# Two of twelve pairs of attention heads move beside the first output layer

## The chip, the cores and the metric

The kernel runs on one core of one Trainium2 chip. Its time is the device time of one execution in microseconds (us); three runs of the kernel before gave 1255.74 to 1256.49 us, with a median of 1256.26 us. The engines of the core are named as the profile names them: PE is the tensor engine (PEld its weight loads), DVE the vector engine, ACT the scalar engine, POOL GpSimd, and SP the engine that issues most of the DMAs.

## The reference

Attention over 4 batches, 12 heads, 448 tokens and a head size of 64 in float32, with scores capped by a tanh, and behind it two expert layers over all 1792 tokens with 768 columns and 2048 hidden columns:

```python
scores = cap * tanh((q @ k.T / sqrt(64)) / cap)
attn = exp(scores - max) / (sum + 1e-9);  x = attn @ v        # as [1792, 768]
h = x @ moe_w_in;   x = (h * cos(h)) @ moe_w_out
h = maximum(x @ moe2_w_in, 0);   out = (h * h) @ moe2_w_out
```

The weights come as float64, q, k and v as float32.

## The kernel before

**Precision.** Each float32 operand is kept as a high part, rounded to float32r, and a low part, the rest. A product of two such operands is three matmuls (`mm3`): high by high, high by low and low by high.

**Windows and stages.** The four batches are taken in two windows of two. A window is eight stages in a row, each a call of `layer` or `layer_out` with 288 expert matmuls of 128 x 448: `layer(True)` makes half of the first layer's hidden columns with the cosine, `layer_out(o_part)` multiplies them into partial sums that wait in the tiles `part`, a second `layer(True)` and `layer_out(o_x)` do the same for the other half and add, which gives x again as two halves; then `layer(False)`, `layer_out(o_part)`, `layer(False)` and `layer_out(o_y)` do the second expert layer and write the output. In this document a stage of the first window is meant where nothing else is said; its eight stages begin at 138.73, 213.97, 273.37, 333.91, 433.60, 527.45, 620.34 and 699.80 us after the span's start, and the next window begins at 768.92 us.

**Banks of PSUM.** `layer(True)` turns over four banks, the two of `bM` and the two of `bA`. `layer_out` uses `bM` alone, one bank for each of the two batches, and so does `layer(False)`. The copy of a finished bank of `layer_out` is on ACT: L613 in `o_part`, L618 in `o_x`, where DVE then adds the first half's sum (L619), rounds (L620), and POOL makes the low half (L621).

**Weights.** All stages of the first window make float32 of the float64 words, one unit after another: 8 units of 128 x 768 in a `layer`, 12 units of 128 x 512 in a `layer_out`. A unit's steps are a DMA (`w_raw`, SP), an absolute value on ACT (L143), four operations on DVE (L144, L145, L146, L149) and an addition on POOL (L152); then its high part on ACT (L166) and its low part on POOL (L169), which the tensor engine waits for. `w_next` begins each unit: it writes the float32 form of the next unit to DRAM for the later window (`w_keep`), splits the next unit, loads the words four units ahead, and queues the steps of the unit three ahead, which `w_step` then issues one by one between the matmuls. In a stage `layer_out`, with 24 matmuls a unit and six steps, that is one step every third matmul.

**Attention.** It works on pairs of heads, 12 pairs for each window. The first window's pairs (0 to 11) come ahead of everything. The second window's pairs (12 to 23) run beside stages of the first window. `a_steps` makes a list of 6 x 12 + 5 = 77 steps of them. Counted from a pair's own first step (six after the last pair's), step 0 holds eight transposes, the making of the halves of q and k, and the loads for the next pair; steps 2 to 5 a score group each, four matmuls, with its tanh; steps 3 to 6 the exponentials with their halves ph (ACT, L394) and pl (DVE, L396), step 3 also the halves of v; steps 5 to 8 the product with v, six matmuls each, which add up in `bA`; step 9 the division by the sums on DVE (`a_out`); step 10 writes the result to DRAM. That makes 48 instructions of the tensor engine a pair. `layer(True)` can't have a product with v beside it, since it uses `bA` itself.

**The order.** All engines get their instructions in the order in which the Python code runs; nothing reorders them. `mm` counts the expert matmuls in `rate[0]` and issues one step of the list `side` after each `rate[1]` of them. In `window` the list is set ahead of `layer_out(o_x)`, with a rate of (1152 - 20) // 77 = 14, so the steps spread over `layer_out(o_x)`, `layer(False)`, `layer_out(o_part)` and `layer(False)`; what is left over runs ahead of the last stage. `later` and `tick` put off the second and third part of a tile's cosine or square by one tile.

Of the kernel before, what the change touches and what calls it, by code (L numbers as in the profile page):

```python
# [21 lines left out]
CAP_MAX = 40.0  # L22
# what a pair of heads makes room for, after each of its four chunks, of the first weights' steps
W_SLOTS = [("act", "dve"), ("act", "dve"), ("pool", "split"), ("dma", "act", "dve")]
# [4 lines left out]
def tile_softcap_attention_moe_cos_moe_relu2(  # L29
# [11 lines left out]
):  # L41
    # Every float32 operand x of a product is carried as hi + lo, both float32r:
    # hi is x rounded to float32r, lo = x - hi, and hi*hi + hi*lo + lo*hi keeps float32's accuracy.
    nc = tc.nc
# [52 lines left out]

# [1 line left out]
    # They come as float64, in two words. The first batch rounds them to float32 from the words,  # L99
    # keeps that in DRAM for the batches after it, and splits it; later batches load and split it.  # L100
    wseq = []
# [27 lines left out]
    def w_bits(i):  # L129
        # The steps that make float32 of the words, the last of them the rounding; or the load of what they made.  # L130
        if i >= wend[0]:
            return []
        n = wseq[i % NW].shape[1] * P
        wf[i] = t = wf_p.tile([P, NCC * P], F32, name="wf", tag="wf")
        f, u = t[:, :n], t[:, :n].bitcast(U32)
        if i >= NW:
            nc.sync.dma_start(out=f, in_=wkeep[i % NW])
            return []
        r = wraw.pop(i)
        rd = wf_p.tile([P, NCC * P], U32, name="wd", tag="wd", bufs=1)  # L140
        lo, hi = r[:, :n, 0], r[:, :n, 1]
        return [
            lambda: nc.scalar.activation(out=f, in_=r.bitcast(F32)[:, :n, 1], func=AF.Abs),  # L143
            lambda: nc.vector.tensor_scalar(out=rd[:, :n], in0=lo, scalar1=2.0 ** -29, scalar2=None, op0=ALU.mult),  # L144
            lambda: nc.vector.tensor_scalar(out=f, in0=f, scalar1=2.0 ** -15, scalar2=None, op0=ALU.max),  # L145
            lambda: nc.vector.tensor_scalar(  # L146
                out=u, in0=u, scalar1=3, scalar2=0x3FFFFFFF, op0=ALU.logical_shift_left, op1=ALU.bitwise_and
            ),
            lambda: nc.vector.scalar_tensor_tensor(  # L149
                out=u, in0=hi, scalar=0xC0000000, in1=u, op0=ALU.bitwise_and, op1=ALU.bitwise_or  # L150
            ),
            lambda: nc.gpsimd.tensor_tensor(out=u, in0=u, in1=rd[:, :n], op=ALU.add),  # L152
        ]
# [26 lines left out]
    def w_start():  # L180
        # The first units' steps, each with the engine that it holds.
        i = wpos[0]
        early = [("dma", partial(w_raw, i)), ("dma", partial(w_raw, i + 1))]
        for j in range(i, i + 4):
            # the steps exist only once the load before them does
            early += [(e, partial(w_bit, j, k)) for k, e in enumerate(("act",) + 4 * ("dve",) + ("pool",))]
# [33 lines left out]

# [1 line left out]
    # Partition r < 64 holds tokens 4r..4r+3, partition r >= 64 tokens 256+3(r-64)..+2;  # L222
    # column 128c + r of a transposed tile is the c-th token of partition r.
    def rows_a(t, b, h, n=1):
# [4 lines left out]

    # The pairs before the first layer find the tiles of g free; later pairs run beside the layers.  # L230
    raws, vraws, qkts = {}, {}, {}
# [13 lines left out]

    # the second pair's loads need not wait for the first's to be consumed
    def wide_view(t):
# [5 lines left out]
    def a_load(n):  # L253
# [5 lines left out]
        else:  # L259
            qr = at_p.tile([P, 4, 2, D], F32, name="qr", tag="qr")  # L260
        # the fourth chunk of k holds one head's tokens in each half, and zeros beside them
        eq, ek = (nc.sync, nc.sync) if n else (nc.scalar, nc.gpsimd)
# [66 lines left out]
    def a_score(n, g):  # L329
# [10 lines left out]
        else:  # L340
            # rows: the high parts of k twice, beside q's high and low parts; then k's low part
            q2, k2, kl = qkts[n]
# [191 lines left out]

# [1 line left out]
    pend = []  # L536
# [93 lines left out]
    def y_tr(b, d, y):  # L630
# [13 lines left out]
        )  # L644

    def window(w, steps=(), weave=None):
        layer(True, weave)
        layer_out(o_part)
        layer(True)
        side[:] = steps  # L650
        if steps:
            rate[:] = [0, (4 * FB * NCC * 3 * WB - 20) // len(steps)]
        layer_out(o_x)
        layer(False)
        layer_out(o_part)
        layer(False)
        while side:
            side_step()
        rate[:] = [0, 0]
        layer_out(o_y(w), w)  # L660

    # |score| <= |cap|, so exp(score) needs no shift while |cap| <= CAP_MAX; and 1e-9 beside the
    # shifted sum, which is at least 1, is below half a unit in its last place. For a larger cap
    # all is computed once more, from scores shifted by their row's maximum.
    def general():
# [19 lines left out]

    # Products of zeros that nothing reads: the tensor engine's clock doubles only after it has been busy a while.
    def busy(n):
# [67 lines left out]
```

## Time and profile before

| | us |
|---|---|
| median of three runs | 1256.26 |
| lowest, highest run | 1255.74, 1256.49 |
| span of the profiled execution (first to last instruction) | 1255.5 |
| PE busy | 1203.0 (96%) |
| DVE busy | 787.4 (63%) |
| ACT busy | 674.4 (54%) |
| POOL busy | 529.9 (42%) |

The busy shares are means over stages that have different limits; the table by stage in the rows below tells them apart. The profiled execution is told by its span alone; the median of the runs is 0.8 us above it. A matmul's duration in the profile overlaps the next one's, so the pace of the tensor engine is read from the length of a stage and not from the mean duration of a matmul.

### The profile page before, as it was taken

How to read it: one execution, taken by the hardware profiler on the slowest of the kernel's cores; microseconds unless marked ns; L12 is line 12 of the kernel's file. 1: busy time of each engine (PE TensorE's matmuls, PEld its weight loads, DVE VectorE, ACT ScalarE, POOL GpSimd, SP SyncE). 2: the span in 40 equal slices, each digit the busy share in tenths (PEclk: the TensorE clock that was granted, in tenths of full speed). 3: DMA queues.
4: the chain of work that ended last, by engine and by line, in shares of the span. 5: the costliest groups of instructions: out<-in, count | busy, mean ns of one | idle time of the engine just before them, and what ended most of it. 6: DMA issues, size and time to landing. Idle time of an engine off the chain costs nothing.

```text
span 1255.5 us, 16524 instructions
## 1 busy us (share of the span) xinstructions
PE 1203.0 (96%) x5931; PEld 1038.6 (83%) x5931; DVE 787.4 (63%) x1123; ACT 674.4 (54%) x1068; POOL 529.9 (42%) x358
## 2 busy tenths in 40 slices
PE   8888889999999899999999989999999999999996
PEld 6555678998878778888888879999999999999996
DVE  6999999669988998777787773530353232013222
ACT  7787576346766688876687434531362144114311
POOL 3555545555566654344443554222224432222221
PEclk9999999999999999999999999999999999999999
DMA  4333243454344443345533465112111211221132
GB/s 106 88 93 97 61 158 122 160 197 143 120 123 139 152 131 122 115 129 153 168 133 111 151 199 145 44 44 66 64 38 51 65 62 35 58 72 46 43 94 49
DMA packets 145308, 130.17 MB, mean 104 GB/s; under 512 B 54816, under 2 KB 124720, under 8 KB 145216
## 3 DMA queue, kind: packets, MB, share of 16 engines
q1 hardware_dynamic: 144224, 128.72, 33.5%
q8 instruction: 49, 0.80, 0.3%
q14 instruction: 43, 0.35, 0.1%
q10 hardware_dynamic: 928, 0.23, 0.1%
q0 software_dynamic: 64, 0.07, 0.0%
HBM read 95.55 MB, written 33.42 MB: 103 GB/s over the span
## 4 chain that ended last, share of the span: by engine, by line
PE 68%; DVE 19%; issue 6%; ACT 3%; DMA 2%; POOL 1%; SPq 1%; DVEq 0%; ACTq 0%; POOLq 0%
PE bM L524 55%; PE bA L524 6%; PE bA L407 3%; PE bS L348 2%; DVE wd L144 2%; DVE g L392 2%; DVE wf L145 2%; DVE xl L96 1%; DVE u L554 1%; DVE st L422 1%; DVE xx L434 1%; DVE wf L146 1%; DVE wf L149 1%; DVE g L570 1%; POOL wf L152 1%
## 5 line engine op out<-in xcount | busy, mean ns | idle before, releaser
L524 PE MATMUL bM<-g,wh 128*128 128x448 f32 x1536 | 445.7, 370 | 6.2 <-DVE part L626 5.1
L169 POOL TENSOR_TENSOR wl<-wf,wh 128x512 fp32r<-128x512 f32 (+1 forms) x160 | 256.3, 1602 | 336.1 <-DVE wh L168 300.3
L524 PEld LDWEIGHTS bM<-g,wh 128*128 128x128 f32 x1536 | 286.7, 189 | 36.0 <-ACT wh L166 4.8
L524 PE MATMUL bM<-g,wl 128*128 128x448 f32 x768 | 284.0, 370 | 5.8 <-POOL wl L169 5.7
L152 POOL TENSOR_TENSOR wf<-wf,wd 128x512 uint32<-128x512 uint32 (+1 forms) x80 | 133.2, 1665 | 234.6 <-issue 129.2
L524 PE MATMUL bM<-xh,wl 128*128 128x448 f32 x576 | 212.2, 368 | 2.7 <-POOL wl L169 2.7
L524 PE MATMUL bM<-xh,wh 128*128 128x448 f32 x576 | 212.3, 369 | 1.3 <-ACT xh L93 1.3
L524 PE MATMUL bM<-xl,wh 128*128 128x448 f32 x576 | 211.6, 367 | 0.2 <-DVE xl L96 0.2
L524 PEld LDWEIGHTS bM<-g,wl 128*128 128x128 f32 x768 | 145.0, 189 | 20.8 <-POOL wl L169 7.2
L570 DVE TENSOR_TENSOR g<-u,g 128x448 fp32r<-128x448 f32 x128 | 91.8, 717 | 73.9 <-ACT g L569 73.9
L144 DVE TENSOR_SCALAR wd<-wr 128x512 uint32<-128x512 uint32 (+1 forms) x80 | 96.7, 1209 | 46.3 <-POOL wf L152 42.0
L168 DVE CAST wh<-wf 128x512 fp32r<-128x512 f32 (+1 forms) x80 | 39.1, 489 | 135.1 <-PE bM L524 121.0
L524 PEld LDWEIGHTS bM<-xh,wl 128*128 128x128 f32 x576 | 108.2, 188 | 14.6 <-POOL wl L169 4.3
L524 PEld LDWEIGHTS bM<-xh,wh 128*128 128x128 f32 x576 | 108.2, 188 | 13.5 <-issue 3.1
L524 PEld LDWEIGHTS bM<-xl,wh 128*128 128x128 f32 x576 | 108.2, 188 | 10.6 <-issue 1.3
L613 ACT COPY part<-bM 128x448 f32<-128x448 f32 x48 | 25.6, 534 | 122.8 <-PE bM L524 122.6
L569 ACT CAST g<-u 128x448 fp32r<-128x448 f32 x128 | 71.7, 560 | 31.3 <-DVE u L559 29.9
L554 DVE SCALAR_TENSOR_TENSOR u<-kk,u 128x448 f32<-128x448 f32 x64 | 53.5, 836 | 54.0 <-ACT kk L553 54.0
L564 ACT ACTIVATE u<-bM 128x448 f32<-128x448 f32 x64 | 34.9, 546 | 78.6 <-PE bM L524 78.4
L166 ACT CAST wh<-wf 128x512 fp32r<-128x512 f32 (+1 forms) x80 | 56.0, 700 | 35.9 <-PE bM L524 32.6
L396 DVE TENSOR_TENSOR pl<-pg,ph 128x896 fp32r<-128x896 f32 (+1 forms) x48 | 58.5, 1219 | 20.6 <-ACT ph L394 20.2
L524 PE MATMUL bA<-xh,wl 128*128 128x448 f32 x186 | 68.5, 368 | 2.2 <-POOL wl L169 2.2
(139 smaller groups left out, 1891.5 us busy)
## 6 DMA issues: line engine op xcount, KB each, us to landing
wr<-in_moe_w_in_dram SPq DMA_DIRECT2D x33, 768.0 KB, 4.5
wr<-in_moe_w_out_dram SPq DMA_DIRECT2D x48, 512.0 KB, 3.5
wkeep<-wf SPq DMA_DIRECT2D x32, 384.0 KB, 2.8
wkeep<-wf SPq DMA_DIRECT2D x48, 256.0 KB, 2.8
wf<-wkeep SPq DMA_DIRECT2D x32, 384.0 KB, 3.0
wf<-wkeep SPq DMA_DIRECT2D x48, 256.0 KB, 2.6
vr<-in_v_dram SPq DMA_DIRECT2D x48, 96.0 KB, 2.4
out_dram<-o SPq DMA_DIRECT2D x24, 128.0 KB, 2.4
```

Source lines behind the costliest of these rows:

```text
L144: lambda: nc.vector.tensor_scalar(out=rd[:, :n], in0=lo, scalar1=2.0 ** -29, scalar2=None, op0=ALU.mult),
L152: lambda: nc.gpsimd.tensor_tensor(out=u, in0=u, in1=rd[:, :n], op=ALU.add),
L166: nc.scalar.copy(out=hi[:, :n], in_=t[:, :n])
L168: nc.vector.tensor_copy(out=hi[:, :n], in_=t[:, :n])
L169: nc.gpsimd.tensor_tensor(out=lo[:, :n], in0=t[:, :n], in1=hi[:, :n].bitcast(F32), op=ALU.subtract)
L396: (nc.gpsimd if slow else nc.vector).tensor_tensor(out=pl[:, :nt], in0=t, in1=ph[:, :nt].bitcast(F32), op=ALU.subtract)
L407: nc.tensor.matmul(acc(n)[j][:, :S], a[:, 3 * j + g, :], x[:, j], start=(g == 0 and i == 0), stop=False)
L524: nc.tensor.matmul(o, l, r, start=start, stop=stop)
L554: nc.vector.scalar_tensor_tensor(out=u, in0=kk, scalar=MAGIC, in1=u, op0=ALU.subtract, op1=ALU.subtract)
L564: nc.scalar.activation(out=u, in_=ps, func=AF.Relu)
L569: nc.scalar.copy(out=gh[b][i], in_=u)
L570: nc.vector.tensor_tensor(out=gl[b][i], in0=u, in1=gh[b][i].bitcast(F32), op=ALU.subtract)
```

## The change

The steps of the later window's attention are cut in two. The first 6 x 2 + 5 = 17 steps run beside the first `layer_out(o_part)`, with a rate of 288 // 18 = 16 expert matmuls a step; whatever of them is left then runs before the second `layer(True)`. These are the pairs 12 and 13 whole, and of pair 14 the transposes, three of four score groups and two of four exponentials. The cut lies ahead of pair 14's first product with v, so `bA` holds nothing of attention while `layer(True)` runs. The other 60 steps run where all 77 ran, with a rate of 1152 // 61 = 18. In the later window there are no steps, and the order of its instructions is as before.

```diff
+    def beside(steps, mms):
+        side[:] = steps
+        rate[:] = [0, mms // (len(steps) + 1)]
+
+    def aside():
+        while side:
+            side_step()
+        rate[:] = [0, 0]
+
     def window(w, steps=(), weave=None):
+        mms = FB * NCC * 3 * WB
+
+        first = 6 * 2 + 5
         layer(True, weave)
+        beside(steps[:first], mms)
         layer_out(o_part)
+        aside()
         layer(True)
-        side[:] = steps
-        if steps:
-            rate[:] = [0, (4 * FB * NCC * 3 * WB - 20) // len(steps)]
+        beside(steps[first:], 4 * mms)
         layer_out(o_x)
         layer(False)
         layer_out(o_part)
         layer(False)
-        while side:
-            side_step()
-        rate[:] = [0, 0]
+        aside()
         layer_out(o_y(w), w)
```

The rest of the diff takes out comments.

## Rows read from the trace of the kernel before

**Rows 1.** The page, section 1: busy time, share of the span, instructions

```profile
PE 1203.0 (96%) x5931; PEld 1038.6 (83%) x5931; DVE 787.4 (63%) x1123; ACT 674.4 (54%) x1068; POOL 529.9 (42%) x358
```

**Rows 2.** Stages: length, PE PEld DVE ACT POOL busy (count), PEclk, DMA, GB/s

```profile
213.97:273.37 59.40, 59.32 (x289) 54.04 (x290) 41.02 (x55) 24.09 (x42) 33.70 (x24) 1.00 0.54 180
273.37:333.91 60.54, 59.27 (x289) 53.94 (x288) 58.21 (x73) 41.69 (x74) 31.92 (x16) 1.00 0.40 137
333.91:433.60 99.69, 92.61 (x436) 76.64 (x434) 91.11 (x120) 67.49 (x98) 60.80 (x45) 0.97 0.43 134
433.60:527.45 93.85, 92.98 (x451) 75.59 (x450) 78.46 (x106) 79.65 (x118) 42.37 (x29) 1.00 0.38 121
527.45:620.34 92.89, 92.89 (x458) 77.42 (x456) 69.33 (x98) 69.94 (x102) 42.15 (x35) 1.00 0.49 150
829.11:887.86 58.75, 58.75 (x290) 54.09 (x288) 7.49 (x16) 8.60 (x16) 16.34 (x12) 1.00 0.21 63
```

**Rows 3.** The same, of line L524 (expert matmuls) alone: PE, PEld

```profile
333.91:433.60 99.69, 66.87 (x290) 54.47 (x288) 0.97 0.43 134
433.60:527.45 93.85, 64.02 (x289) 52.69 (x288) 1.00 0.38 121
527.45:620.34 92.89, 63.82 (x290) 52.69 (x288) 1.00 0.49 150
```

**Rows 4.** Waits of PE in layer_out(o_x), first 31 us, then the rest: us, times, longest

```profile
PE bM L524 <- POOL wl L169: 2.5, 2, 1.8
PE bS L348 <- DVE q L309: 1.3, 1, 1.3
...
PE bM L524 <- POOL wl L169: 3.2, 1, 3.2
```

**Rows 5.** Windows in layer_out(o_x) behind the two bunches of waits

```profile
358.93:362.34 3.41, 3.41 (x11) 3.06 (x10) 2.25 (x3) 0.97 (x2) 2.27 (x3) 0.50 0.21 63
427.20:430.60 3.40, 3.40 (x11) 3.02 (x10) 3.37 (x6) 0.91 (x2) 1.98 (x1) 0.50 0.16 48
```

**Rows 6.** Groups of DVE in layer_out(o_x): busy us, mean ns, idle before

```profile
L396 DVE TENSOR_TENSOR pl<-pg,ph 128x896 fp32r<-128x896 f32 (+1 forms) x12 | 14.1, 1174 | 0.1
...
L305 DVE TENSOR_TENSOR kl<-bS,k 64x512 fp32r<-64x512 f32 x8 | 5.5, 686 | 0.7 <-ACT q L301 0.6
L309 DVE TENSOR_TENSOR q<-bS,q 64x448 fp32r<-64x448 f32 x8 | 5.0, 622 | 0.1
L422 DVE STREAM_TRANSPOSE st<-bA 64x448 f32<-64x448 f32 x4 | 2.6, 648 | 0.0
L434 DVE TENSOR_TENSOR xx<-bA,st 64x448 f32<-64x448 f32 x4 | 2.5, 617 | 0.1
...
L326 DVE CAST vh<-vr 128x448 fp32r<-128x448 f32 x3 | 1.8, 608 | 0.0
...
L428 DVE STREAM_TRANSPOSE st<-rc 128x448 f32<-128x448 f32 x2 | 1.3, 645 | 0.1
...
L427 DVE RECIPROCAL rc<-st 128x14 f32<-128x14 f32 x2 | 0.5, 242 | 0.1
```

**Rows 7.** Timeline of DVE, opening of the first layer_out(o_part), then of layer_out(o_x)

```profile
220.91 0.68 DVE L149 SCALAR_TENSOR_TENSOR wf<-wr,wf 128x512 uint32<-128x512 uint32 x1
221.63 0.63 DVE L570 TENSOR_TENSOR g<-u,g 128x448 fp32r<-128x448 f32 x1
...
342.65 1.38 DVE L305 TENSOR_TENSOR kl<-bS,k 64x512 fp32r<-64x512 f32 x2
344.04 1.26 DVE L309 TENSOR_TENSOR q<-bS,q 64x448 fp32r<-64x448 f32 x2
345.33 0.69 DVE L149 SCALAR_TENSOR_TENSOR wf<-wr,wf 128x512 uint32<-128x512 uint32 x1
```

**Rows 8.** Timeline of ACT in layer_out(o_x): the table load and what follows

```profile
345.38 1.28 ACT L354 ACT_TABLE_LOAD   x1 [0.41 <-DVE q L309]
346.67 1.01 ACT L354 ACTIVATE pg<-bS,tsc 128x896 f32<-128x896 f32 x1
```

## Prediction

> **What bounds the kernel now.** I read the page first: the tensor engine is busy 96% of the span [rows 1], so all that any reordering can win is in its idle 4%. The table of stages comes next. A stage is one call of `layer` or `layer_out`, 288 expert matmuls each (counted off in the trace). The later window's first `layer_out` has nothing beside it and takes 58.75 us, 204 ns a matmul, with no gap [rows 2]: that is the floor of a stage. The second `layer_out(o_part)` of the first window carries attention and takes 92.89 us; (92.89 - 58.75) / 168 attention instructions (458 - 290) = 0.203 us each, at a fully busy engine [rows 2, 3]. So attention costs the tensor engine 0.203 x 48 = 9.75 us a pair wherever it stands, and a stage's loss is its length - 58.75 - 0.203 x (its attention instructions):
> - first `layer_out(o_part)`, no attention: 59.40 - 58.75 = 0.65 us
> - second `layer(True)`, none: 60.54 - 58.75 = 1.79 us
> - `layer_out(o_x)`, 436 - 290 = 146: 99.69 - 58.75 - 29.64 = 11.30 us
> - first `layer(False)`, 451 - 289 = 162: 93.85 - 58.75 - 32.89 = 2.21 us
> - second `layer_out(o_part)`, 168: nothing
>
> [rows 2, 3]. So 16 us are lost in the stretch that the change rearranges, two thirds of them in `layer_out(o_x)`. The waits of the tensor engine tell where in it: in its first 31 us 2.5 us on the low part of a weight (POOL, L169) and 1.3 us on the first pair's q (DVE, L309); later one wait of 3.2 us on L169 [rows 4]. After both bunches the granted clock is at 0.50, the 1.2 GHz level, for 3.4 us [rows 5]; at most 11 instructions stand in each of these stretches, some of them across its edge, where 16.7 would fit at 204 ns: 10 x 0.204 = 2.0 us of work in 3.4, about 1.4 us lost each time. 2.5 + 1.3 + 3.2 + 2 x 1.4 = 9.8 of the 11.3 us. What is late behind L169 is DVE, which is busy 91.1 of 99.7 us there, against 69.3 of 92.9 in the second `layer_out(o_part)` and 41.0 of 59.4 in the first [rows 2]: VectorE makes the weights, adds the halves of x and splits the attention, all in one queue.
>
> **The change part by part.** No matmul is added or taken away: 576 attention instructions stand in other stages at the same 0.203 us, a term of zero. What moves is which stage has them. With a step every 288 // 18 = 16 expert matmuls, steps 0 to 16 run in the first `layer_out(o_part)`: pairs 12 and 13 whole (96 instructions), and of pair 14 the transposes and three score groups (8 + 12), 116 in all; the last step is at matmul 272, so the flush behind it finds nothing. The other 60 steps come every 1152 // 61 = 18 matmuls where 77 came every 14, and end at 1080, as before (1078).
>
> (a) `layer_out(o_x)` has steps 17 to 32 in place of 0 to 19. By the list of steps: the rest of pair 14 (28 instructions), pairs 15 and 16 (48 each) and 12 of pair 17, so 136 for 146. On DVE a pair costs kl 2 x 0.686 + q 2 x 0.622 + vh 0.608 + pl (14.1 us for three pairs) 4.70 + transposes 2 x 0.648 + 0.645 + reciprocal 0.242 + xx 2 x 0.617 = 11.3 us [rows 6]. Before, the stage held two whole pairs, a third without its 3.4 us of output steps and the kl and q of a fourth: 22.6 + 7.9 + 2.6 = 33.1 us. After: pl of two groups and output of pair 14 (1.8 + 3.4), one whole pair, one without output, one kl and q: 5.2 + 11.3 + 7.9 + 2.6 = 27.0 us. DVE loses 6.1 us, the tensor engine 10 x 0.203 = 2.0, so DVE's surplus falls by 4.1 us. DVE's need is then 91.1 - 6.1 = 85.0 against a floor of 58.75 + 27.6 = 86.4 us: it is no longer above it. Less certain is how this falls on single waits. The opening one on q (1.3) goes, since pair 15's transposes come at matmul 36 with its scores at 72, 36 matmuls apart, not 28; the 3.2 us wait late in the stage and its clock dip become less likely; the opening waits on L169 stay in part, as DVE still has the cosine's last tiles in front. Bounds: 0 (all waits come back in new places) and -11.3 (as clean as the second `layer_out(o_part)`). I take -5.0: the 4.1 and about half of a clock dip.
>
> (b) The first `layer_out(o_part)` gets attention at the place where `layer_out(o_x)` lost 2.5 + 1.3 + 1.4 = 5.2 us in its opening. It opens with the same queue of cosine tiles: its last L570 is over at 222.3, 8.3 us after the start. Three things are easier: no halves of x are added on DVE and POOL; the transposes come at matmul 16, behind the fourth unit's L149, which is issued at 15, where at 14 they came ahead of it (in `layer_out(o_x)` kl and q, 2.6 us, stand in front of L149, and so of that unit's POOL steps) [rows 7]; and scores follow 32 matmuls later, not 28. Kl and q then end at about 221.6 + 2.6 = 224.2, the scores are due at about 213.97 + 48 x 0.204 + 1.0 = 224.8. Behind them L570 ends at 224.9, while its tile is due at matmul 46, about 224.2: 0.7 us. Over the stage DVE has 41.0 + 2 x 11.3 + 5.6 (pair 14: kl, q, vh, two pl) = 69 us in 59.4 + 116 x 0.203 = 83 us, 83% (75% in the second `layer_out(o_part)`, which lost nothing). What is queued behind a late tanh on ACT is the copy of a finished bank (L613), and the tensor engine is back at that bank 12 matmuls, 2.4 us, later; one step in three now lands just there (48 = 3 x 16). Bounds: 0 and +5.2. I take +1.5: the 0.7 and one late bank.
>
> (c) The second `layer(True)` lost 1.8 us with DVE busy 58.2 of 60.5 [rows 2]. In the stage ahead a weight unit now lasts some 7 us and not 4.9, and weights are made three units ahead, so it starts with them further ahead in time; against that come pl of pair 14 (1.2 us) and a reload of the sine's table. Bounds -1.8 and +2.5 (both on the path); I take -0.5.
>
> (d) Two table loads on ACT are added, sine in the second `layer(True)` and tanh/exp in `layer_out(o_x)` again, 1.28 us each, with the next instruction starting 0.01 us behind one [rows 8]. ACT is busy 41.7 of 60.5 and 67.5 of 99.7 us there [rows 2], which hides them; uncovered 2.6. I take 0.2. The Trainium skill (ScalarE: Activation LUTs, What ACT_TABLE_LOAD costs) gives a switch a drain of about 1.38 us beside the load, 2.66 us in all; the row shows the load alone, and by the page the term would be at most 5.3 us, and the sum an even time.
>
> (e) The first `layer(False)` has fewer steps for its length: its 2.2 us lie at its start, left over from the stage before. Bounds -2.2 and 0; I take -0.8.
>
> The SP queue: loads of q and k (6) and v (4) now also go through it between the weights' in the first `layer_out(o_part)`; DMA is 54% busy there [rows 2], and the loads for pair 15 land ahead of the second `layer(True)`. No term.
>
> Sum: -5.0 + 1.5 - 0.5 + 0.2 - 0.8 = -4.6 us. The profiled span is 1255.5, so 1250.9; the median of the runs shown is 1256.26, 0.8 above the span: **1251.7 us**.
>
> **The rivals.** *The waits only move* (1253.7 to 1258.8, around 1256). For it: a pair costs DVE 11.3 us and the tensor engine 9.75, so at any rate of steps DVE falls behind in `layer_out(o_x)`, and its opening still has the cosine's tiles; (a) gives 2 or 3 us and (b) and (d) take them. Against it: DVE's total there falls below the floor.
>
> *The first output layer gets the opening of `layer_out(o_x)`* (slower, about 1260). Place: its third and fourth weight units, whose L169 stands on POOL behind L152, which waits for DVE behind kl, q and pl. Price: the 5.2 us of the other opening, clock dip included, and 1.3 in (c) as the lag is handed into a stage with DVE nearly full, against -3.0 left of (a) and (e): +3.5. It decides if L169 of the third unit ends later than about 226, or if the tanh of a step holds the bank's copy by more than 2.4 us. Against it: the order at matmul 15 and 16, and that the second `layer_out(o_part)` shows no wait at all with more attention.
>
> *All the loss goes*: -10 from (a), -2 from (e), -1 from (c), +1.5 from (b): about 1245; for it the clean second `layer_out(o_part)`, against it x's halves.
>
> **How the numbers follow.** Forecast 0.42 (1248.8 to 1253.7), all gone 0.15, only moved 0.25, slower 0.18. A difference under 0.2% (2.5 us) can't be told from none. Faster 0.42 + 0.15 = 0.57, same 0.25, slower 0.18. The range, 1246.5 to 1259.5, cuts about a third of the clean case and somewhat more of the slower one.
>
> **What would show it.** In the stages of the new profile: `layer_out(o_x)` at 58.75 + 27.6 + about 6 = 92 to 93 us, with no wait on L309; the first `layer_out(o_part)` at 83 + 2 = about 85; the second `layer(True)` at 60; six table loads in place of four. Wrong would be a first `layer_out(o_part)` over 88 us, a second `layer(True)` over 62, or DVE's waits in `layer_out(o_x)` as long as now.

## The result, and the profile after

The changed kernel takes 1266.84 us (median of 4 runs, 1266.31 to 1268.05) against 1256.38 for the kernel before: a ratio of 1.0086, 95% interval 1.0072 to 1.0100. It is slower by 10.5 us, where 4.6 us less were forecast. Its profiled execution has a span of 1264.5 us. The counts of the page are those of [rows 1] but for two more instructions on ACT, the added table loads:

```profile
PE 1205.6 (95%) x5931; PEld 1040.6 (82%) x5931; DVE 790.4 (63%) x1123; ACT 674.5 (53%) x1070; POOL 531.9 (42%) x358
```

The stages from the first `layer_out(o_part)` to the second `layer(False)`, columns as in [rows 2]:

```profile
213.88:299.12 85.24, 83.22 (x404) 69.43 (x404) 61.77 (x92) 60.18 (x89) 40.89 (x33) 1.00 0.50 152
299.12:359.92 60.80, 59.38 (x289) 54.08 (x290) 58.49 (x73) 42.73 (x75) 31.88 (x16) 1.00 0.42 141
359.92:465.43 105.51, 92.59 (x426) 75.89 (x424) 84.94 (x113) 58.20 (x87) 56.49 (x42) 0.95 0.40 123
465.43:550.90 85.47, 85.23 (x418) 71.76 (x417) 75.56 (x94) 71.49 (x108) 42.89 (x26) 1.00 0.39 121
550.90:635.56 84.66, 83.79 (x410) 70.27 (x409) 57.89 (x87) 56.62 (x83) 39.59 (x32) 1.00 0.49 154
635.56:709.81 74.25, 74.25 (x366) 65.11 (x365) 62.86 (x79) 53.82 (x87) 34.91 (x20) 1.00 0.40 136
```

Read with the prediction's floor (58.75 us and 0.203 us for each attention instruction), the losses are:

| stage | attention before, after | loss before | loss after |
|---|---|---|---|
| first `layer_out(o_part)` | 0, 116 | 0.65 | 2.9 |
| second `layer(True)` | 0, 0 | 1.8 | 2.05 |
| `layer_out(o_x)` | 146, 136 | 11.3 | 19.1 |
| first `layer(False)` | 162, 128 | 2.2 | 0.7 |
| second `layer_out(o_part)` | 168, 120 | 0 | 1.5 |
| second `layer(False)` | 100, 76 | 0.4 | 0.1 |

That is 10.0 us more, and 7.8 of it in `layer_out(o_x)`, which has ten instructions fewer beside it and is 5.8 us longer. What PE waits for there (us in total, times, longest; against [rows 4]):

```profile
PE bM L524 <- POOL wl L169: 8.5, 4, 3.1
PE bA L407 <- DVE u L559: 3.9, 1, 3.9
PE bM L524 <- ACT u L618: 0.5, 2, 0.3
```

The second and the third row are new, and the wait on q of [rows 4] is gone, as foretold. The second group of steps begins in the middle of pair 14: its first step, at matmul 18, opens with a product with v, whose second matmul goes into bank `bA[1]`. The layer before has just ended, and DVE still reads that bank for the cosine's last tile. PE's timeline and then DVE's show it (start, us):

```profile
363.69 0.47 PE L407 MATMUL bA<-ph,vh 128*128 128x448 f32 x1
368.06 0.74 PE L407 MATMUL bA<-ph,vh 128*128 128x448 f32 x1 [3.90 <-DVE u L559]
```

```profile
367.39 0.62 DVE L559 TENSOR_TENSOR u<-bA,u 128x448 f32<-128x448 f32 x1
367.93 0.68 DVE L149 SCALAR_TENSOR_TENSOR wf<-wr,wf 128x512 uint32<-128x512 uint32 x1
370.62 1.09 DVE L396 TENSOR_TENSOR pl<-pg,ph 128x896 fp32r<-128x896 f32 x1 [2.01 <-ACT ph L394]
373.43 0.63 DVE L570 TENSOR_TENSOR g<-u,g 128x448 fp32r<-128x448 f32 x1 [1.72 <-ACT g L569]
```

While PE stands, the steps behind it come late (ACT's L394 waits for that product, and DVE's L396 for L394), and DVE, the busiest engine of this stage after PE, has nothing to do:

```profile
369.65 0.94 ACT L394 CAST ph<-pg 128x896 fp32r<-128x896 f32 x1 [1.94 <-PE bA L407]
```

In the stage's first 22 us DVE is busy 15.0 us; in the same stretch of the kernel before it was busy 20.6. The two rows, after and then before, and DVE's waits in that stretch of after:

```profile
359.92:381.92 22.00, 17.82 (x80) 14.73 (x79) 15.03 (x24) 15.82 (x26) 7.19 (x6) 0.92 0.26 77
```

```profile
333.91:355.91 22.00, 19.91 (x95) 15.82 (x93) 20.57 (x30) 17.34 (x26) 11.87 (x10) 1.00 0.38 117
```

```profile
DVE pl L396 <- ACT ph L394: 2.6, 2, 2.0
DVE kl L305 <- ACT q L301: 2.4, 1, 2.4
DVE g L570 <- ACT g L569: 1.7, 1, 1.7
```

The granted clock falls to 0.50, the 1.2 GHz level, three times in the stage where it fell twice [rows 5], as the waits of 3.9, 3.1 and 3.1 us end:

```profile
367.68:371.09 3.41, 3.02 (x9) 2.29 (x9) 1.40 (x3) 0.96 (x2) 1.28 (x1) 0.50 0.34 96
405.22:408.64 3.42, 3.42 (x10) 3.04 (x10) 1.98 (x4) 1.72 (x3) 1.64 (x2) 0.50 0.13 27
456.42:459.84 3.42, 3.42 (x10) 3.00 (x10) 3.38 (x6) 0.65 (x1) 1.46 (x2) 0.50 0.01 4
```

In the first `layer_out(o_part)` the longest wait stands at its very end, ahead of the next stage's first matmul, on a bank's copy that ACT makes late (L613); the first row below is that one, the others are in its opening:

```profile
PE bM L524 <- ACT part L613: 1.3, 1, 1.3
PE bM L524 <- DVE u L559: 0.9, 1, 0.9
PE bM L524 <- DVE g L570: 0.7, 1, 0.7
```

### The profile page after: what moved, and what is told of

Read it like the earlier page. It is cut to its first block, busy times and chain, and to the rows that moved or that the text cites. A ratio compares the mean times of both kernels' runs of the same rounds, so it can differ in the third digit from the quotient of the medians.

```text
span 1264.5 us, 16515 instructions
## 1 busy us (share of the span) xinstructions
PE 1205.6 (95%) x5931; PEld 1040.6 (82%) x5931; DVE 790.4 (63%) x1123; ACT 674.5 (53%) x1070; POOL 531.9 (42%) x358
## 4 chain that ended last, share of the span: by engine, by line
PE 67%; DVE 20%; issue 5%; ACT 2%; SPq 2%; POOL 2%; DMA 1%; DVEq 0%; POOLq 0%; ACTq 0%
PE bM L524 54%; PE bA L524 5%; PE bA L407 3%; PE bS L348 3%; DVE wd L144 3%; DVE u L554 2%; DVE g L392 2%; DVE wf L145 1%; DVE wf L146 1%; DVE g L570 1%; DVE xl L96 1%; DVE u L559 1%; DVE st L422 1%; DVE wf L149 1%; DVE xx L434 1%
## 5 line engine op out<-in xcount | busy, mean ns | idle before, releaser
L524 PE MATMUL bM<-g,wh 128*128 128x448 f32 x1536 | 445.7, 371 | 8.2 <-DVE part L626 5.1
L169 POOL TENSOR_TENSOR wl<-wf,wh 128x512 fp32r<-128x512 f32 (+1 forms) x160 | 256.2, 1601 | 345.3 <-DVE wh L168 300.4
L524 PEld LDWEIGHTS bM<-g,wh 128*128 128x128 f32 x1536 | 284.6, 188 | 40.7 <-issue 5.0
L524 PE MATMUL bM<-g,wl 128*128 128x448 f32 x768 | 282.5, 368 | 8.5 <-POOL wl L169 8.5
L152 POOL TENSOR_TENSOR wf<-wf,wd 128x512 uint32<-128x512 uint32 (+1 forms) x80 | 135.1, 1689 | 217.1 <-issue 115.4
L524 PE MATMUL bM<-xh,wh 128*128 128x448 f32 x576 | 213.7, 371 | 3.4 <-ACT xh L93 2.1
L524 PE MATMUL bM<-xh,wl 128*128 128x448 f32 x576 | 211.5, 367 | 1.9 <-POOL wl L169 1.9
L524 PE MATMUL bM<-xl,wh 128*128 128x448 f32 x576 | 211.4, 367 | 0.4 <-POOL xl L621 0.2
L524 PEld LDWEIGHTS bM<-g,wl 128*128 128x128 f32 x768 | 144.6, 188 | 22.5 <-POOL wl L169 10.0
L570 DVE TENSOR_TENSOR g<-u,g 128x448 fp32r<-128x448 f32 x128 | 102.3, 799 | 77.5 <-ACT g L569 77.3
L144 DVE TENSOR_SCALAR wd<-wr 128x512 uint32<-128x512 uint32 (+1 forms) x80 | 96.9, 1211 | 44.4 <-POOL wf L152 31.6
L524 PEld LDWEIGHTS bM<-xh,wh 128*128 128x128 f32 x576 | 108.2, 188 | 17.7 <-issue 3.3
L524 PEld LDWEIGHTS bM<-xh,wl 128*128 128x128 f32 x576 | 108.4, 188 | 12.4 <-POOL wl L169 3.3
L524 PEld LDWEIGHTS bM<-xl,wh 128*128 128x128 f32 x576 | 108.4, 188 | 9.8 <-POOL xl L621 0.6
L613 ACT COPY part<-bM 128x448 f32<-128x448 f32 x48 | 25.4, 531 | 111.0 <-PE bM L524 110.8
L564 ACT ACTIVATE u<-bM 128x448 f32<-128x448 f32 x64 | 34.9, 545 | 76.0 <-PE bM L524 73.0
L143 ACT ACTIVATE wf<-wr 128x512 f32<-128x512 f32 (+1 forms) x80 | 61.2, 765 | 21.6 <-DMA wr<-in_moe_w_out_dram 13.1
L524 PE MATMUL bA<-xh,wl 128*128 128x448 f32 x186 | 68.8, 370 | 2.2 <-POOL wl L169 2.2
L524 PE MATMUL bA<-xl,wh 128*128 128x448 f32 x186 | 68.5, 369 | 0.0
```

Of the source, the lines that this page charges most:

```text
L169: nc.gpsimd.tensor_tensor(out=lo[:, :n], in0=t[:, :n], in1=hi[:, :n].bitcast(F32), op=ALU.subtract)
L524: nc.tensor.matmul(o, l, r, start=start, stop=stop)
L564: nc.scalar.activation(out=u, in_=ps, func=AF.Relu)
L570: nc.vector.tensor_tensor(out=gl[b][i], in0=u, in1=gh[b][i].bitcast(F32), op=ALU.subtract)
```

## The experiments

"o_x" is `layer_out(o_x)` of the first window, "the next layer" the first `layer(False)`. Losses are by the floor above, from each run's profiled execution. The table holds what the text below draws on; the kernel before took 1256.3 to 1256.9 us beside these runs.

| run | attention in o_x | length of o_x | loss o_x + next layer | median, us | ratio to before |
|---|---|---|---|---|---|
| before | 146 | 99.7 | 13.5 | 1256.4 | |
| after | 136 | 105.5 | 19.8 | 1266.84 | 1.0086 |
| e5 nothing beside o_x | 0 | 76.1 | 17.3 | 1264.63 | 1.0065 |
| e13 four later, 17 | 96 | 94.9 | 19.5 | 1265.84 | 1.0066 |
| e12 whole pairs, 17 | 112 | 93.1 | 16.4 | 1259.48 | 1.0022 |
| e15 whole pairs, 14 | 146 | 99.7 | 12.6 | 1255.04 | 0.9986 |
| e16 whole pairs, 11 | 194 | 109.6 | 14.5 | 1257.85 | 1.0007 |
| e14 before, 11 | 194 | 109.6 | 13.7 | 1257.79 | 1.0008 |
| e17 after, 14 | 168 | 104.7 | 14.1 | 1259.71 | 1.0028 |
| e18 after, 14, two later | 144 | 96.9 | 10.7 | 1255.68 | 0.9995 |

**First theory: the bank wait, and the queue of POOL behind it.** e1 puts four empty steps ahead of the second group, so that the product with v comes behind the cosine.

```diff
-        beside(steps[first:], 4 * mms)
+        beside([[] for _ in range(4)] + steps[first:] if steps else [], 4 * mms)
+        rate[1] = 18
```

> The kernel after, with four empty steps ahead of the second group of 60, at the same 18 matmuls a step, so that pair 14's first product with v comes at matmul 90 of layer_out(o_x) and not at 18. Theory 1 (the bank): in the kernel after, that product waits 4.2 us for bank bA, which the cosine's last tile (DVE, L559) still reads 8 us into the stage, and all expert matmuls stand behind it; a clock dip follows. Then this wait and its dip go, some 5 us: layer_out(o_x) falls from 105.5 to about 99 us (it also has four steps less in it), the total to about 1261. Rival (load): what costs is that attention is in full flow from the stage's first matmul, so that DVE's lag brings the waits on L169; then the wait at the opening only changes its name, and the total stays within 2 us of 1266.8.

Measured: 1270.25 us (1265.46 to 1271.12), ratio 1.0112 (1.0096 to 1.0129). The expectation failed. The profiled execution is the fastest of the four, 1265.46, and its losses hold for that one alone: the wait on `bA` is gone and o_x lost 9.3 us, but the next layer lost 6.7, most of it at its start (PE waits 2.9 us for L620, 1.1 for L621). The list of 64 steps at 18 now ends with the last `layer(False)`'s last matmul, and the `layer_out(o_y)` behind it takes 71.3 us in place of 69.1. So the edit changed three things at once: the wait, the end of the list, and the opening of o_x, which now has nothing beside it (the price of that stands with e13).

e2 (on after) and e3 (on before) put the low half of x (L621) off by one tile, so that POOL need not wait for DVE's L620; e4 is e2 with e1's steps.

```diff
+        later(0, o_xl, b, d, t)
+
+    def o_xl(b, d, t):
         nc.gpsimd.tensor_tensor(out=xl[b][d], in0=t, in1=xh[b][d].bitcast(F32), op=ALU.subtract)
```

> The kernel after, with the POOL instruction of layer_out(o_x) that makes the low half of x (L621) put off by one tick, so that it is issued behind the next weight unit's low half (L169) and not ahead of it. Theory 2 (POOL's order): the waits of the tensor engine on L169 in layer_out(o_x) (0.8, 3.2, 1.8 and 3.2 us, and two clock dips) come because L169 stands behind L621, which waits for DVE's addition behind the attention's steps. Then most of these go, 8 to 10 us: total about 1257 to 1259; the 4.2 us wait of pair 14's product stays. Rival (load): DVE makes the weights too late itself (L149), and L169 would be late without L621 ahead of it: under 3 us gained.

> The kernel before with the same putting off of L621. Theory 2: its waits on L169 in layer_out(o_x) of 1.8 and 3.2 us and both clock dips go, 5 to 8 us: total about 1249 to 1251. Rival (load): no more than 2 us.

> The kernel after with both edits. If theories 1 and 2 both hold, their gains add: about 1266.8 - 5 - 9 = 1253, and layer_out(o_x) has no wait over 1 us. If it then stands no lower than the kernel before with L621 put off, moving the two pairs has no gain of its own even with its two faults mended.

Measured: 1267.24 (1.0086), 1258.28 (1.0013, 1.0003 to 1.0022) and 1271.45 (1.0123). In none of the three did the theory's time come. o_x's loss fell to 11.0, 8.8 and 9.6 us, and that of the next layer rose to 9.7, 5.8 and 10.8: a wait taken out of o_x came up behind it.

**Is it DVE's load?** e6 (on before) and e7 (on after) give the rounding of x (L620) to ACT.

```diff
-        nc.vector.tensor_copy(out=xh[b][d], in_=t)
+        nc.scalar.copy(out=xh[b][d], in_=t)
```

> The kernel before, with the rounding of x in layer_out(o_x) (L620, 12 times, 0.4 to 1.9 us each) on ACT in place of DVE. Theory 3: DVE has 8 us less to do in the stage that it bounds, so the loss there falls from 11.3 to 4 to 6 us: total about 1250. Rival (the order of the queues, not DVE's load): ACT now waits for DVE's addition with all that is queued behind it, and the total is 1256 or more.

> The kernel after with the same move of L620 to ACT. Theory 3: some 5 to 7 us off, about 1260 to 1262. If the kernel after is held by waits of DVE for ACT and the tensor engine (its DVE is idle for 20 of 112 us there) and not by DVE's work, under 3 us, or worse, as ACT gets more.

Measured: 1264.8 (1.0066) and 1269.27 (1.0106), both slower than what they start from. DVE has less to do, and o_x loses 16.9 and 17.2 us: ACT's copies of the banks (L618) come late instead, six waits and 7.0 us in all in e6. Less work on DVE alone doesn't shorten this stage.

**The stage alone.** e5 leaves o_x with no attention at all; the second group begins at the next layer.

```diff
-        beside(steps[first:], 4 * mms)
         layer_out(o_x)
+        beside(steps[first:], 3 * mms)
```

> The kernel after with nothing beside layer_out(o_x): the second group of 60 steps starts with layer(False), at 864 // 61 = 14 matmuls a step. Theory 3 (DVE's own work and its handshake with POOL fill layer_out(o_x) whether or not attention is there: some 65 us of work without attention, 8 us of waits that the weights need, against 58.75 us of matmuls, of which about 7 may be left over for the next stage): layer_out(o_x) alone then still loses 6 to 8 us of the tensor engine, and the total is about 1256. Rival (what I predicted with: it is the attention that puts DVE over the floor): the stage loses under 2 us, and the total is about 1249.

Measured: 1264.63 (1.0049 to 1.0082), a miss in its size. o_x, then PE's waits in it:

```profile
360.37:436.49 76.12, 66.08 (x290) 58.43 (x289) 64.02 (x78) 24.59 (x42) 49.71 (x34) 0.91 0.43 142
```

```profile
PE bM L524 <- POOL wl L169: 10.0, 6, 3.2
```

With nothing beside it, o_x still takes 76.1 us, not 58.75, and DVE is busy only 64.0 of them. Of the 17.3 us lost, 10.0 are PE's waits; and for 13.7 us the granted clock is at 0.50, which by an estimate (half of that stretch) costs another 6.8. Its twelve weight units go round between DVE and POOL (DVE waits 9.0 us for L152). In the middle of the stage, at the full clock, two units take 11.97 us, from one L152 of POOL to the next but one, so 6.0 us a unit, while PE needs 4.9:

```profile
394.06 1.29 POOL L152 TENSOR_TENSOR wf<-wf,wd 128x512 uint32<-128x512 uint32 x1 [1.15 <-issue]
406.03 1.30 POOL L152 TENSOR_TENSOR wf<-wf,wd 128x512 uint32<-128x512 uint32 x1 [1.15 <-issue]
```

Attention fills part of that time: the 146 instructions of the kernel before lengthen the stage by 99.7 - 76.1 = 23.6 us, 0.162 each in place of 0.203. About half of these 6 us are waits (7.0 in place of 10.0), the rest the clock, at 0.50 for 6.8 us there in place of 13.7.

**The same wait in the kernel before.** e8 adds one unread matmul into `bA[1]` at matmul 18 of o_x.

```diff
         rate[0] += 1
+        if rate[1] and rate[0] == 18:
+            nc.tensor.matmul(bA[1][:, :S], xl[0][0][:, 0:P], xl[0][0], start=True, stop=True)
```

> The kernel before with one more matmul, whose product nothing reads, into the second bank of bA at matmul 18 of layer_out(o_x), so that the tensor engine waits there for the cosine's last tile as in the kernel after, and nothing else is changed. Theory 1 (the bank): some 4 us of wait at the opening; DVE runs dry behind it since the attention and the stage's first sums come late, and the total rises by 4 to 8 us. Theory 3: DVE is behind anyway and works on during the wait, so that later waits on L169 shrink by as much, and the total rises by under 2 us.

Measured: 1256.97 (0.9994 to 1.0013). PE's waits in o_x (lines behind the added one are two higher):

```profile
PE bA L528 <- DVE u L561: 3.9, 1, 3.9
PE bM L524 <- POOL wl L169: 3.2, 1, 3.2
```

The wait of 3.9 us stands there and costs nothing that can be measured: DVE has the weights, kl and q in its queue, is idle 2.4 us in the first 22, and the waits of [rows 4] in the opening, 3.8 us, are gone: the new wait stands in their place.

**Order of the weight's steps, and x on DVE.** e9 (on before) and e11 (on after) issue L144 as the last of DVE's four steps; e10 (on before) gives L621 to DVE.

```diff
-            lambda: nc.vector.tensor_scalar(out=rd[:, :n], in0=lo, scalar1=2.0 ** -29, ...),    # L144
...
+            lambda: nc.vector.tensor_scalar(out=rd[:, :n], in0=lo, scalar1=2.0 ** -29, ...),
```

```diff
-        nc.gpsimd.tensor_tensor(out=xl[b][d], in0=t, in1=xh[b][d].bitcast(F32), op=ALU.subtract)
+        nc.vector.tensor_tensor(out=xl[b][d], in0=t, in1=xh[b][d].bitcast(F32), op=ALU.subtract)
```

> The kernel before with one of the four DVE steps of a weight unit (L144, which writes the single tile wd that POOL's L152 reads) issued last of the four, right ahead of L152, in all stages of the first window; everything is computed as before. Theory 4 (layer_out(o_x) is bound by the round of DVE and POOL through the weights and x, one waiting for the other: DVE's L144 waits 6.4 us there for the last unit's L152): these waits go, and the loss of 11.3 us falls by 3 to 6: total 1250 to 1253. Rival: the round only turns differently, DVE waits elsewhere and the total stays within 2 us of 1256.3.

> The kernel before with the low half of x in layer_out(o_x) (L621) made by DVE in place of POOL. Theory 4 (the round through both engines, with DVE's copies held up while POOL runs: L620 takes 0.39 us alone and up to 1.9): POOL has 16 us less and one handing over less stands ahead of L169, so in spite of 7 us more on DVE the loss in the stage falls by 2 to 5 us: total 1251 to 1254. Theory 3 (DVE's load alone is the bound): the loss rises by 5 to 7 us, total about 1262.

> The kernel after with the same order of L144. Theory 4: 3 to 7 us off, about 1260 to 1263; the two pairs' move still loses against the kernel before with this order. Rival: within 2 us of 1266.8.

Measured: 1258.68 (1.0016), 1257.02 (1.0001) and 1270.48 (1.0109). In e9 and e10 o_x loses 6.5 and 8.2 us in place of 11.3 and the next layer 6.5 and 5.2 in place of 2.2: the sums, 13.0 and 13.4, are those of the kernel before, 13.5. The loss comes up one stage later and is not removed. e10 lies between its two theories; e9 and e11 are slower than what they start from, and part of that is in the first window's `layer_out(o_y)`, whose weights are made in the new order too: 71.9 and 73.5 us in place of 69.1.

**Whole pairs.** e12 cuts between pairs: 12 and 13 alone beside the first `layer_out(o_part)`, pairs 14 to 23 from their own beginning, 65 steps at 17.

```diff
-    def a_steps(w):
+    def a_steps(w, s0, s1):
...
-        beside(steps[:first], mms)
+        beside(steps[0], mms)          # a_steps(w + 1, 0, 2)
...
-        beside(steps[first:], 4 * mms)
+        beside(steps[1], 4 * mms)      # a_steps(w + 1, 2, NA)
```

> The kernel after with the cut between pairs: 17 steps of pairs 12 and 13 alone beside the first layer_out(o_part), then pairs 14 to 23 from their own first step (65 steps, one every 17 matmuls), so that layer_out(o_x) opens as in the kernel before and no pair is half done in between. If the cut through pair 14 (its product with v at matmul 18, its halves due at once) is what costs, the loss in layer_out(o_x) and layer(False) together falls from 19.8 to about 14 us, as in the kernel before (13.5), and the total is about 1260: what then remains is the 2 us of the first layer_out(o_part) and 1 or 2 later. Rival (layer_out(o_x) loses more the less attention it has beside it, with 17.4 us at none): about 16 us in the two stages, total about 1263.

Measured: 1259.48, ratio 1.0022 (1.0012 to 1.0031): 7.4 us better than after. The first `layer_out(o_part)` loses 1.3, the second `layer(True)` 0.6; o_x and the next layer still lose 16.4, so the time is the theory's and the loss of these two stages the rival's. Between this kernel and after, two things differ: the cut and the pace. The next runs part them.

**Pace in o_x.** e13 is e1 at 17, so that the list ends where it did. e14 is the kernel before at 11 matmuls a step in o_x and 16 behind; e15 and e16 are e12 at 14 and 18, and at 11 and 21.

```diff
+        rate[1] = 14
         layer_out(o_x)
+        rate[1] = 18
```

> The kernel after with four empty steps ahead of its second group, at 17 matmuls a step so that the list still ends where it ended. The first product of pair 14 with v then comes behind the stretch in which cosine's last tile is read. Theory (the cut through pair 14 costs through the bank wait and a VectorE that has nothing to do for the next steps): the 4.2 us wait and VectorE's 7 us of idle time in the first 22 us of o_x go, and the kernel takes about 1263 us. Rival (what is lost in o_x and the layer(False) behind it is set by their whole round of VectorE and POOL work, and a wait removed early in it only comes up later): within 2 us of 1266.8.

> The kernel before with its list at 11 matmuls a step for the first 26 steps in o_x, then 16, so more attention lies beside o_x and less beside the layer behind it. Theory (o_x lasts 76 us by its own round, and TensorE has room there that attention fills for nothing): the loss of o_x and the first layer(False) together falls from 13.5 to about 12 us, the time by 1 to 2 us, to about 1255. Rival (the prediction's step: attention is what makes VectorE late in o_x): 3 us or more above before, at 1259.5 or later.

> Two whole pairs beside the first output layer, the other ten in the old place, now at 14 matmuls a step while o_x runs and at 18 behind it. Theory (the 3.0 us that o_x and the layer behind it lost with two pairs fewer is the attention that o_x no longer has beside it): 1256.5 to 1257.5, level with before. Rival (it is something else in moving pairs): 1259.5, as with an even 17.

> As the kernel with whole pairs at 14 and 18, with 11 matmuls a step in o_x and 21 behind it. If o_x takes attention for nothing up to what it held before and beyond, this is at or below before, 1254.5 to 1256.5; if VectorE becomes the bound at this density, it is above the run at 14, 1258 or later.

Measured: e13 1265.84 (1.0050 to 1.0081): the rival's number, with runs from 1262.83 to 1267.01. The wait on `bA` is gone, and o_x loses 16.7 us all the same. Its waits up to the next layer's first matmul, then those of its first 22 us alone, and a stretch of low clock that begins in the last of these:

```profile
PE bM L524 <- POOL wl L169: 7.4, 5, 3.2
PE bM L524 <- ACT u L618: 3.5, 1, 3.5
```

```profile
PE bM L524 <- POOL wl L169: 4.3, 3, 3.2
378.84:385.67 6.83, 5.72 (x15) 5.12 (x16) 5.26 (x7) 2.25 (x3) 3.56 (x3) 0.50 0.34 116
```

With four empty steps o_x has nothing beside it up to matmul 85, and it opens as it does in e5 and e1, with 4.3 us of waits (4.4 in those) where after had the one of 3.9. PE's waits in o_x fall only from 12.9 to 10.9 us, and over o_x and the next layer the clock is at 0.50 for 17.1 us in place of 10.2 (in e1's profiled execution it stayed at 1.00 through o_x, behind the same waits in the opening). So e13 put other waits in the place of the one that it took away, and doesn't tell what that one costs at 17. e12, at 17 too, has attention beside it from matmul 17 on, and is 6.4 us faster.

e14 1257.79 (0.9999 to 1.0018): between the two; 48 more instructions beside o_x lengthen it by 9.9 us, 0.207 each, so at 14 there is nothing left to fill. e15 1255.04, ratio 0.9986 (0.9977 to 0.9995), below what either side expected and the one run of these that beats both kernels, by 1.8 us against before. e16 1257.85 (0.9998 to 1.0016), close to its rival's 1258 and 2.8 us above e15, so 11 is too dense. The stages of e15 from the first `layer_out(o_part)` to the next layer:

```profile
213.69:293.29 79.60, 78.89 (x384) 67.24 (x385) 58.18 (x87) 51.47 (x77) 38.87 (x30) 1.00 0.51 159
293.29:352.66 59.37, 59.00 (x289) 54.02 (x288) 56.05 (x71) 43.09 (x75) 31.57 (x16) 1.00 0.41 138
352.66:452.35 99.69, 92.60 (x435) 76.59 (x434) 91.12 (x120) 67.45 (x98) 60.76 (x45) 0.97 0.44 134
452.35:537.61 85.26, 84.70 (x414) 70.58 (x412) 72.06 (x93) 69.57 (x104) 41.39 (x27) 1.00 0.41 130
```

At 14, with pairs from their beginning, o_x is that of the kernel before to 0.01 us [rows 2], waits and clock included, whichever pairs they are. Against e12, only the pace differs: 1259.48 - 1255.04 = 4.4 us.

**The cut and the pace parted.** e17 is after at 14 in o_x and 20 behind it; e18 is after with two empty steps ahead of the second group, at 14 and 19.

```diff
-        beside(steps[first:], 4 * mms)
+        beside([[] for _ in range(2)] + steps[first:] if steps else [], 4 * mms)    # e18 alone
+        rate[1] = 14
         layer_out(o_x)
+        rate[1] = 20    # e18: 19
```

> The kernel after, cut through pair 14 as it is, at 14 matmuls a step while o_x runs and 20 behind it, so that the list ends at matmul 1080 as before. The pace in o_x is that of the kernel before and of the run with whole pairs at 14, so only the cut is left as a difference to the latter. If the cut itself costs (the bank wait, and a VectorE with nothing ready behind it): o_x and the first layer(False) together still lose 16 us or more, the time is 1262 or later. If the pace of 18 was what cost: they lose about 13, and the time is about 1258, what remains being the first o_part and the second layer(True).

> As the kernel after at 14 and 20, with two empty steps ahead of the second group (14 and 19), so that pair 14's first product with v comes behind the stretch in which cosine's last tile is read. If the bank wait is what the cut costs, this is 3 to 5 us under the run without the empty steps, at 1258 to 1259; if a removed early wait only comes up later, it is within 1.5 us of it.

Measured: e17 1259.71 (1.0017 to 1.0038), between its two answers, so both count; e18 1255.68 (0.9986 to 1.0004), 4.0 us under it, the difference that was expected for the bank wait, at a lower time than the 1258 to 1259 that was named. e17's o_x, PE's waits in it, and DVE's in its first 22 us:

```profile
359.72:464.43 104.71, 96.44 (x458) 79.31 (x457) 87.24 (x122) 70.75 (x103) 58.98 (x43) 0.97 0.41 126
```

```profile
PE bA L407 <- DVE u L559: 4.7, 2, 3.9
PE bM L524 <- ACT u L618: 1.9, 1, 1.9
PE bM L524 <- POOL wl L169: 1.7, 1, 1.7
```

```profile
DVE pl L396 <- ACT ph L394: 5.8, 2, 3.2
DVE kl L305 <- ACT q L301: 2.4, 1, 2.4
DVE g L570 <- ACT g L569: 1.3, 1, 1.3
```

o_x is no longer than in after (104.7 against 105.5) though 32 more attention instructions stand beside it, 6.5 us of PE: they fill time that PE waited for L169 (8.5 us in after, 1.7 here), and the stages behind are rid of them. In e18, o_x, PE's waits in it and DVE's in its opening:

```profile
359.80:456.72 96.92, 91.23 (x434) 74.65 (x433) 86.92 (x119) 63.66 (x93) 58.52 (x43) 0.98 0.43 131
```

```profile
PE bM L524 <- POOL wl L169: 5.3, 4, 2.4
PE bA L407 <- DVE pl L396: 0.2, 1, 0.2
```

```profile
DVE wd L144 <- POOL wf L152: 1.2, 1, 1.2
```

The wait of 3.9 us on `bA` and DVE's waits behind it, 9.5 us in e17, are gone. The first step comes at matmul 42, and in the first 22 us PE waits for L169 only once, 0.6 us. The granted clock is at 0.50 for 3.4 us of o_x, and for 6.8 in e17. e18 also has 24 attention instructions fewer beside o_x; no run takes that apart from the wait.

**The sum.** After 1266.84; the pace of 14 takes 7.1 off (e17), the two empty steps, and with them the bank wait, another 4.0 (e18), and what is left is 1255.68, level with 1256.57 before (1256.38 beside after). So the cut itself and the two pairs in their new place cost nothing together: by the floor, the first `layer_out(o_part)` and the second `layer(True)` lose 2.5 us more in e18 than before, o_x and the next layer 2.8 less. The pace of 18 and the place at which pair 14's first product lands make up the 10.5 us, taken away in this order. What the bank wait costs alone, at 18, is open: no run has two empty steps at that pace, and e1 and e13 leave the opening empty. Nor does a run show whether 18 costs by being wide or by its rhythm, since the weights' steps in o_x also stand on multiples of three; e12, at 17, loses 4.4 us to e15.

## Why the prediction was wrong

The step that failed is (a), -5.0 us for `layer_out(o_x)`; it measured +7.8.

- (a) DVE's work did fall by what was worked out: from the stage's start to the last rounding of x, it was busy 97.4 us before and 91.0 after, 6.4 less against 6.1 foretold. Its idle time in the same stretch rose from 8.7 to 20.7. The argument set a sum of DVE's busy time against PE's floor, as if DVE had only to get through its list. e5 shows a stage that lasts 76 us with nothing beside it, with DVE idle for 12 of them, 9.0 of these in waits for POOL's L152. From 146 attention instructions to none the stage gives back 0.162 us for each, and beside a stage that loses nothing they cost 0.203. A wider pace was counted as relief, and was a price of 7.1 us (e17). The wait of 3.2 us late in the stage was to become less likely; two of 3.1 us came.
- (a) also listed what the first steps hold by name ("the rest of pair 14") and did not ask what the first of them needs at matmul 18. The front matter said that `layer(True)` uses `bA` itself; its last reader is DVE, 8 us into the next stage. That is the other 4.0 us (e18).
- (b) was mis-sized by 0.8: +2.3 for the first `layer_out(o_part)` against +1.5. The 0.7 on L570 stands there as foretold; the late copy of L613 was the one late bank, 1.3 us.
- (c) -0.5 was foretold, +0.25 came; with whole pairs it was -1.2 (e12).
- (d) Six loads, hidden but for what (c) and the opening of o_x hold; no run takes them out alone. In e15 they are there too, and its second `layer(True)` and o_x are no longer than before. In after, the load in o_x begins at 365.37, takes 1.28 us, and the next ACTIVATE begins at 366.66. The Trainium skill (ScalarE: Activation LUTs, What ACT_TABLE_LOAD costs) counts 2.66 us for a switch, so 5.3 us at most for the two, by an estimate; e15 doesn't bear that out.
- (e) -0.8 foretold, -1.5 measured, but the second `layer_out(o_part)` lost 1.5 us where it had lost nothing, 0.9 of it in one wait on ACT's L564, 3.6 us after its start; no term had that.
- The rival that the first output layer would inherit the opening was wrong (2.9 us there, not 5). Slower had a chance of 0.18, but on that rival's account; the forecast had no rival in which `layer_out(o_x)` itself becomes slower, which is why the range ended at 1259.5.

## What to carry to other kernels

Before thinning the work beside a stage, find how long the stage lasts with nothing beside it: if two other engines go round in it longer than the tensor engine needs, work beside it is partly free and moving it away is a cost. When a list of steps is cut, ask of the first step behind the cut which buffer it needs at the matmul where it lands, and who reads that buffer last. A wait is not priced by its length: 3.9 us cost nothing measurable in e8, where they stood in the place of others, and about 4 us in e17, where DVE stood idle behind them. And an edit that takes a wait away by leaving a gap has to be read for the waits that the gap lets in (e1, e13).

## What was not expected of the hardware

Most of DVE's additions and copies between tiles of SBUF (the tiles that are neither banks of PSUM nor in DRAM) take longer while POOL runs. The same L619 took 0.62 us at 394.51 and 2.27 us here, beside POOL's L152, and L620 0.39 us clear of POOL and 1.92 beside it (DVE's timeline of after, then POOL's):

```profile
450.41 2.27 DVE L619 TENSOR_TENSOR part<-u,part 128x448 f32<-128x448 f32 x1
452.72 0.39 DVE L620 CAST xh<-part 128x448 fp32r<-128x448 f32 x1
469.65 1.92 DVE L620 CAST xh<-part 128x448 fp32r<-128x448 f32 x1
```

```profile
449.51 2.69 POOL L152 TENSOR_TENSOR wf<-wf,wd 128x768 uint32<-128x768 uint32 x1
```

In o_x of after, L145 took 0.45 us in seven calls clear of POOL and 1.38 in five beside it (means). Not all do: the cast L326 took 0.61 us at 435.09, beside POOL's L621, and as much clear of POOL; kl and q, which DVE reads from PSUM, took 0.69 and 0.62 in o_x of the kernel before in either case. The Trainium skill (SBUF — State Buffer, SBUF: two separate sides) says that an instruction of DVE with two inputs in SBUF, or in a mode with two ports, and one of GpSimd that reads SBUF take a shared pair of ports by turns, each for a whole instruction; the durations of L619, L620 and L145 agree with it. So DVE's busy time holds waiting for POOL, which is a second reason why its sum says little about what a stage needs.
